# Backward attention: scores and dP on four 32-row strips, one dP tile in 32 multiplied by GpSimd

## The chip, the cores and the metric

One core of a Trainium2 chip runs the whole program in one launch. Time is the device time of one execution in microseconds; the figure compared is the median over runs. The engines are named as the profile names them: PE (TensorE matmul), PEld (its weight loads), DVE (VectorE), ACT (ScalarE), POOL (GpSimd) and SP (SyncE, which here issues DMAs). PSUM is the memory that PE writes; "crossbar" is the DMA path that transposes 128x128 blocks while it copies.

## The reference

The kernel computes the output and nine gradients of a transformer block with adaptive layer norm: x has 2048 tokens of 512 features, attention has 32 heads of 16 features. Cut to the part that the change touches:

```python
def _A_ref(x, wqkv, wo):            # x: 1 x 2048 x 512, H = 32, Dh = 16
    q, k, v = ...                   # each 1 x 32 x 2048 x 16
    scores = jnp.einsum('bhqd,bhkd->bhqk', q, k) * Dh ** (-0.5)
    p = _softmax(scores, axis=-1)
    o = jnp.einsum('bhqk,bhkd->bhqd', p, v)
    return o.transpose(0, 2, 1, 3).reshape(B, S, D) @ wo
...
_out, _vjp = jax.vjp(_f, A_x, A_wqkv, A_wo, B_w1, B_b1, B_w2, B_b2, c, w_mod)
_grads = _vjp(grad_out)
```

The backward pass of attention needs, for each head, the scores again, P = exp(scores) (a division by the row sum is folded into other operands), dP = dO V^T minus the row term, dS = P * dP, and from these dV = P^T dO, dK = dS^T Q and dQ = dS K.

## The kernel before

The program runs in three parts: the forward pass with the MLP and its backward work in the background (`phase_fwd`), the backward pass of attention (`phase5`, with the loops in `attn_bwd`), and the weight gradients and the input gradient (`phase6`). The change lies in `attn_bwd` and in the functions that set up its operands.

**Loops.** The 32 heads form eight groups of four (`g`), each of two pairs (`jp`), and a pair has two heads (`a`). For one pair, `c` runs over four stretches of 512 keys and `ib` over 16 blocks of 128 queries. One (`g`, `jp`, `c`, `ib`) is a *unit*: two tiles of 128 queries by 512 keys, one for each head. There are 8 x 2 x 4 x 16 = 1024 units. Four units in a row (`G` = 4) are a *group* with one `ds` tile of 128 x (4 x 2 x 512); a pair has 16 groups, and there are 256 of them.

**One unit.** For each head `a`:

1. PE multiplies the scores `st` (L1555). Q lies transposed with four heads in 128 partitions, head j in partitions 32j and up. The other operand `masked["KT"][j]` holds K of one head in its rows and zeros elsewhere, and the matmul takes 64 rows.
2. PE multiplies `dp` (L1494) of the unit before, from `dOT` and `masked["VT"][j]`, whose heads lie two strips further on, so that it uses the opposite 64 rows. It has 18 rows a head: 16 features and two for the row term.
3. ACT takes the exponential of `st` into `pu` (L1559).
4. DVE multiplies `dp` by `pu` into `ds` (L1496).

`st` and `dp` have three PSUM buffers each, `pu` six, `ds` three and `dsT` four.

**Behind it.** `dS` puts the unit on the list `pend`; at every second unit `kv_two` takes two units from there and accumulates dK and dV in `acckv` (L1448), two units at four to five units' distance. dQ needs dS with keys in the partitions. That is `dsT`, 32 blocks of 128x128 for a group. The first four blocks (unit 0, head 0) are turned by PE (`turn_ds`, L1513) and copied out of PSUM by ACT (L1514) once the third unit of the group is under way; the other 28 are turned by the crossbar in one DMA that SP issues when the group's last product is done (L1504). `dq` (L1470) takes its units from the list `pendq` two groups later. When a stretch of keys is done ACT copies `acckv` to `kvT` (L1451), and after a pair `turn` transposes that on PE, into an `st` buffer, and ACT copies it out (L1459, L1463).

**Loads.** POOL issues the loads of the next pair and the next group (`pair_pieces`, `load_group`), one for a group of units and 14 in most pairs. Each is preceded by a one-element copy `tick` (L1543) that reads an element of `ds` and so holds POOL until DVE has got there. `pair_pieces` loads K and V of the next pair into the rows of the masked tiles; their other rows were set to zero once, in `open_bwd` (L1375).

**Order.** PE, SP and POOL run in the order in which the program was written, DVE and ACT in the scheduler's.

Of the kernel before, what the change touches and what calls it, by code (L numbers as in the profile page):

```python
# [9 lines left out]
BF16 = mybir.dt.bfloat16  # L10
F32 = mybir.dt.float32
ACT = mybir.ActivationFunctionType
ALU = mybir.AluOpType
# [6 lines left out]
P = 128  # L20
DH = 16
# [84 lines left out]
class K:  # L106
# [1249 lines left out]
    def open_bwd(self):  # L1356

        nc = self.nc
        S, ST, D, DT = self.S, self.ST, self.D, self.DT
        self.open_pool("pad_r", bufs=1, side="right").tile([P, 240], BF16, name="pad_r")  # L1360
        xp = self.open_pool("p5x", bufs=1, side="right")
        self.wp = self.open_pool("p5w", bufs=1, side="right")
        cp = self.open_pool("p5c", bufs=1, side="right")
        m01 = xp.tile([P, 4 * S], BF16, name="m01")
        self.q0 = xp.tile([P, 2 * S + 3 * ST * 4 * DH], BF16, name="q0")
        self.xhat1_6 = m01[:, :ST * D].rearrange("p (st d) -> p st d", d=D)
        self.wq_6 = self.q0[:, :3 * DT * D].rearrange("p (kt n) -> p kt n", n=3 * D)
        nc.vector.memset(self.kvs[0:64], self.scale)
        nc.vector.memset(self.kvs[64:P], 1.0)
        m23 = cp.tile([P, 4 * S], BF16, name="m23")  # L1370
        self.masked = {n: [m[:, (2 * t + a) * S:(2 * t + a + 1) * S] for m in (m01, m23) for a in range(2)]
                       for t, n in enumerate(("KT", "VT"))}
        for ms in self.masked.values():
            for m in ms:
                nc.vector.memset(m, 0.0)  # L1375
        self.qp = self.open_pool("p5q", bufs=1, side="right")
        self.Tq = {}

# [35 lines left out]
    def pair_pieces(self, g, jp):  # L1414
        pieces = []
        for n, src, sh, rows in (("KT", self.KTq_d, 0, DH), ("VT", self.VTq_d, 2, DH + 2)):
            for j in (2 * jp, 2 * jp + 1):
                r = 32 * ((j + sh) % 4)
                pieces.append((self.masked[n][j][r:r + rows, :], src[g, r:r + rows, :]))
        return pieces  # L1420

    def attn_bwd(self):
# [7 lines left out]
        tc, nc = self.tc, self.nc  # L1430
        S, D, H, NQ, ST, SC = self.S, self.D, self.H, self.NQ, self.ST, self.SC
        G = 4
# [3 lines left out]
        acckv = accp.tile([P, 512], F32, name="acckv")  # L1436
        nc.vector.memset(acckv[:], 0.0)
        accq = accp.tile([P, ST, 2, DH], F32, name="accq")
        masked, kvs = self.masked, self.kvs
        pend, pendq = [], []  # L1440

        def kv(u):
# [10 lines left out]
        def turn(g, jp, kvT, s0):  # L1453

            h0 = 4 * g + 2 * jp
            n = ST // 2
            tp = stp.tile([P, n, P], BF16, name="st")
            for st in range(n):
                nc.tensor.transpose(tp[:, st, :], kvT[:, (s0 + st) * P:(s0 + st + 1) * P], self.ident[:])  # L1459
            v = tp[:].rearrange("p s (t a e) -> p t s a e", t=2, a=2)  # L1460
            for t, dst in enumerate((self.dk_t, self.dv_t)):
                d = dst[:, s0:s0 + n, h0 * DH:(h0 + 2) * DH].rearrange("p s (a d) -> p s a d", a=2)
                nc.scalar.copy(d, v[:, t, :, :, 0:DH])  # L1463
# [15 lines left out]
        def kv_two(n=2):  # L1479
            for u in pend[2 - n:2]:  # L1480
                kv(u)
            (T, g, jp, c, ib, kvT, pu, ds) = pend[1]
            del pend[:2]
            if c % 2 and ib == ST - 1 and (g, jp) == (NQ - 1, 1):
                turnq.append((g, jp, kvT, 4 * (c - 1)))
            elif c == SC - 1 and ib == ST - 1:
                turnq.extend((g, jp, kvT, s0) for s0 in (0, ST // 2))

        def dP(u, a):

            (T, g, jp, c, ib, kvT, pu, dsg, i, grp) = u
            rd = slice(64 - 64 * jp, 128 - 64 * jp)
            dp = dpp.tile([P, 512], F32, name="dp")
            nc.tensor.matmul(dp[:], lhsT=T["dOT"][rd, ib * P:(ib + 1) * P],  # L1494
                             rhs=masked["VT"][2 * jp + a][rd, 512 * c:512 * (c + 1)], start=True, stop=True)
            nc.vector.tensor_tensor(dsg[:, i, a], dp[:], pu[:, a, :], ALU.mult)  # L1496

        def dS(u):

            (T, g, jp, c, ib, kvT, pu, dsg, i, grp) = u  # L1500
            pend.append((T, g, jp, c, ib, kvT, pu, dsg[:, i]))
            if i == G - 1:
                dsT = grp[0]
                nc.sync.dma_start_transpose(dsT[:, 4:, :], dsg[:].rearrange("p i a k -> p (i a k)")[:, 512:])  # L1504
                for i in range(G):
                    pendq.append((T, g, jp, c, ib - G + 1 + i, i, dsT))

        def turn_ds(dsg, grp):

            dsT = dtp.tile([P, 8 * G, P], BF16, name="dsT")  # L1510
            tp = stp.tile([P, 4, P], BF16, name="st")
            for b in range(4):
                nc.tensor.transpose(tp[:, b, :], dsg[:, 0, 0, b * P:(b + 1) * P], self.ident[:])  # L1513
            nc.scalar.copy(dsT[:, 0:4, :], tp[:])  # L1514
            grp.append(dsT)

        tick = self.tick
        T = self.T0
        turnq, last = [], None
        for g in range(NQ):  # L1520
            for jp in range(2):
                if jp == 0:
                    if g + 1 < NQ:
                        Tn, later = self.load_group(g + 1)
                    else:
                        Tn, later = None, self.wq_pieces(1) + self.load_wmt()
                    cut = len(later) // 2 if Tn else len(later)
                    pieces = self.pair_pieces(g, 1) + later[:cut]
                    later = later[cut:]
                elif g + 1 < NQ:  # L1530
                    pieces = self.pair_pieces(g + 1, 0) + later
                else:
                    pieces = [(self.xhat1_6[:, st, :], self.xhat1_d.rearrange("(st p) d -> p st d", p=P)[:, st, :])
                              for st in range(ST)]
                kvT = kvp.tile([P, S], BF16, name="kvT")
                total = len(pieces)
                for c in range(SC):
                    c0 = 512 * c
                    for ib0 in range(0, ST, G):
                        m = c * (ST // G) + ib0 // G  # L1540
                        while pieces and (total - len(pieces)) * SC * ST <= m * G * total:
                            if last:
                                nc.gpsimd.tensor_copy(tick[:], last[7][0:1, 0, 0, 0:1])  # L1543
                            nc.gpsimd.dma_start(*pieces.pop(0))
                        dsg, grp = self.dsp.tile([P, G, 2, 512], BF16, name="ds"), []
                        for i in range(G):
                            ib = ib0 + i
                            q = slice(ib * P, (ib + 1) * P)
                            if turnq and i == 2:
                                turn(*turnq.pop(0))  # L1550
                            pu = self.pup.tile([P, 2, 512], BF16, name="pu")
                            for a in range(2):
                                stt = stp.tile([P, 512], F32, name="st")
                                rs = slice(64 * jp, 64 * jp + 64)
                                nc.tensor.matmul(stt[:], lhsT=T["QT"][rs, q], rhs=masked["KT"][2 * jp + a][rs, c0:c0 + 512],  # L1555
                                                 start=True, stop=True)
                                if last:
                                    dP(last, a)
                                nc.scalar.activation(pu[:, a, :], stt[:], ACT.Exp, scale=self.scale)  # L1559
                            if last:  # L1560
                                dS(last)
                            last = (T, g, jp, c, ib, kvT, pu, dsg, i, grp)
                            if i % 2 == 1 and len(pend) >= 4:
                                kv_two()
                            elif i % 2 == 0 and len(pendq) > 2 * G:
                                for _ in range(4 if len(pendq) > 3 * G else 2):
                                    dq(pendq.pop(0), [0, 1])
                            if i == 2:
                                turn_ds(dsg, grp)
            T = Tn  # L1570
        with tc.manual_schedule(engines=ALL):
            for t in (2, 0):
# [338 lines left out]
```

The softmax here doesn't subtract the row's maximum and nothing guards it: scores larger than these inputs give would overflow.

## Time and profile before

| | |
|---|---|
| median of 3 runs | 2569.79 us (2552.87 to 2571.11) |
| span of the profiled execution | 2562.0 us |
| what lies around the span, median less span | 7.8 us |
| PE, PEld busy over the span | 2483.2 us (97%), 1227.4 us (48%) |
| DVE, ACT, POOL busy over the span | 1767.4 us (69%), 2314.2 us (90%), 569.5 us (22%) |
| products `ds` on DVE (L1496) | 2048, from 1180.6 us to 2437.7 us, 677 ns each |
| exponentials `pu` on ACT (L1559) | 2048, 612 ns each |
| crossbar transfers (L1504) | 256, 6.7 us from issue to landing (median), 8.8 at most |
| granted PE clock | 0.994 |

No time of the profiled execution other than its span is recorded; the median stands for it. Busy time counts from an instruction's start to its end, and instructions of one engine overlap by about a tenth of a microsecond, so that an engine that is 97% busy can still have room: the distance from start to start of like instructions shows what it can do. "Idle before" in a group's row is time in which the engine stood still ahead of such an instruction, with what it waited for. The DMA share is a mean over 16 DMA engines and can exceed 1, since packets overlap.

### The profile page before, as it was taken

The page shows a single profiled execution, that of the slowest core. Times are in us where ns is not written, and L with a number is a line of the kernel's source. Part 1 is how long each engine was busy: PE and PEld are TensorE (multiplying, and loading weights), DVE is VectorE, ACT ScalarE, POOL GpSimd, SP SyncE. Part 2 cuts the span into 40 slices and gives each one's busy share as a digit, 9 for nine tenths or more (in the row PEclk, how much of TensorE's full clock was granted, in tenths as well). Part 3 has the DMA queues.
Part 4 walks back from the last instruction along what each step waited for, and adds up shares of the span by engine and source line. Part 5 has one row for each costly group of instructions (what it writes and reads, how often), then busy time and mean ns, then how long its engine had stood idle before and what let it go on. Part 6 is the DMA issues. An engine that isn't in the chain of part 4 may idle for free.

```text
span 2562.0 us, 77852 instructions
## 1 busy us (share of the span) xinstructions
PE 2483.2 (97%) x31239; PEld 1227.4 (48%) x31239; DVE 1767.4 (69%) x3651; ACT 2314.2 (90%) x3757; POOL 569.5 (22%) x1137
## 2 busy tenths in 40 slices
PE   8999899999999999899999999999999999999998
PEld 4555555555555554663444444444444444444443
DVE  6222323323322344667999999999999999999957
ACT  7999999999999996436999999999999999999935
POOL 3554521320221131353011111111111111111223
PEclk9999999999999999999999999999999999999999
DMA  4588742450351153799999999999999999999997
GB/s 165 118 180 196 173 95 83 100 113 22 112 128 49 39 143 113 154 190 211 205 205 202 199 200 201 203 204 200 197 199 198 208 201 197 201 201 229 213 202 191
DMA packets 1193040, 425.37 MB, mean 166 GB/s; under 512 B 1138004, under 2 KB 1161686, under 8 KB 1192678
## 3 DMA queue, kind: packets, MB, share of 16 engines
q1 hardware_dynamic: 1153542, 319.25, 64.2%
q0 software_dynamic: 37056, 100.11, 13.1%
q8 instruction: 244, 4.00, 0.6%
q10 hardware_dynamic: 2080, 1.05, 0.1%
q14 instruction: 118, 0.97, 0.1%
HBM read 73.73 MB, written 62.40 MB: 53 GB/s over the span
## 4 chain that ended last, share of the span: by engine, by line
PE 67%; ACT 20%; DMA 5%; issue 4%; POOL 2%; DVE 1%; SPq 1%; POOLq 0%; DVEq 0%; ACTq 0%
PE st L1555 20%; ACT pu L391 16%; PE acckv L1448 11%; PE accq L1470 8%; PE st L388 7%; PE accbank L322 3%; PE dp L1494 3%; ACT pu L1559 2%; PE st L1513 2%; PE dps L1047 2%; PE pps L1234 2%; PE dp L1604 1%; PE st L1699 1%; DMA dsT<-ds 1%; DMA ev_tm<-ev_fm 1%
## 5 line engine op out<-in xcount | busy, mean ns | idle before, releaser
L1496 DVE TENSOR_TENSOR ds<-dp,pu 128x512 bf16<-128x512 f32 x2048 | 1236.2, 679 | 13.1 <-PE dp L1494 10.2
L1559 ACT ACTIVATE pu<-st 128x512 bf16<-128x512 f32 x2048 | 1073.7, 612 | 46.4 <-PE dp L1494 22.5
L391 ACT ACTIVATE pu<-st 128x1024 bf16<-128x1024 f32 x992 | 912.1, 1077 | 4.6 <-PE st L388 4.4
L388 PE MATMUL st<-QTm,KTq 128*128 128x512 bf16 x1984 | 588.6, 377 | 19.5 <-ACT pu L391 6.0
L322 PEld LDWEIGHTS <-pu 128*128 128x128 bf16 x8192 | 347.5, 96 | 236.1 <-issue 3.1
L322 PE MATMUL accbank<-Vaug,pu 128*128 128x17 bf16 x8192 | 357.7, 171 | 1.2 <-ACT Vaug L522 0.9
L1494 PE MATMUL dp<-m,q 64*128 64x512 bf16 x1024 | 345.7, 382 | 1.1 <-DVE g2w L1053 0.7
L1494 PE MATMUL dp<-m,dOTg 64*128 64x512 bf16 x1024 | 344.6, 381 | 0.1
L1470 PEld LDWEIGHTS <-dsT 128*128 128x128 bf16 x8192 | 239.5, 96 | 213.8 <-issue 209.7
L1555 PE MATMUL st<-m,q 64*128 64x512 bf16 x1024 | 319.5, 382 | 9.2 <-ACT pu L1559 7.5
L1555 PE MATMUL st<-m,QTg 64*128 64x512 bf16 x1024 | 318.9, 381 | 9.5 <-ACT pu L1559 7.8
L388 PEld LDWEIGHTS <-KTq 128*128 128x128 bf16 x1984 | 188.3, 96 | 176.9 <-issue 125.5
L1543 POOL COPY tick<-ds 1x1 bf16<-1x1 bf16 x223 | 39.6, 178 | 1005.4 <-DVE ds L1496 1005.4
L1448 PE MATMUL acckv<-ds,q 128*16 128x512 bf16 x1024 | 154.0, 381 | 0.0
L1448 PE MATMUL acckv<-pu,dOg 128*16 128x512 bf16 x1024 | 154.0, 381 | 0.0
L1448 PE MATMUL acckv<-ds,Qg 128*16 128x512 bf16 x1024 | 154.0, 381 | 0.0
L1448 PE MATMUL acckv<-pu,q 128*16 128x512 bf16 x1024 | 154.0, 381 | 0.0
L1514 ACT COPY dsT<-st 128x512 bf16<-128x512 bf16 x256 | 152.4, 595 | 1.0 <-PE st L1513 1.0
L1470 PE MATMUL accq<-Kg,dsT 128*128 128x16 bf16 x4096 | 143.3, 170 | 3.4 <-DMA dsT<-ds 3.4
L1470 PE MATMUL accq<-q,dsT 128*128 128x16 bf16 x4096 | 143.6, 170 | 0.4 <-DMA dsT<-ds 0.3
L302 POOL DMA_DIRECT2D QTm<-QTq_d x124 | 63.3, 512 | 341.3 <-PE st L388 320.2
L329 DVE RECIPROCAL rl<-accbank 128x4 f32<-128x4 f32 x128 | 22.9, 179 | 162.6 <-PE accbank L322 162.5
(379 smaller groups left out, 2864.8 us busy)
## 6 DMA issues: line engine op xcount, KB each, us to landing
KTq<-KTq_d POOLq DMA_DIRECT2D x24, 512.0 KB, 3.9
duT_d<-auT POOLq DMA_DIRECT2D x3, 1792.0 KB, 7.8
aT_d<-rT POOLq DMA_DIRECT2D x3, 1792.0 KB, 11.1
KTq_d<-KTq SPq DMA_DIRECT2D x32, 128.0 KB, 2.0
QTq_d<-ev_fm SPq DMA_DIRECT2D x32, 128.0 KB, 3.9
VTq_d<-vT POOLq DMA_DIRECT2D x4, 1024.0 KB, 6.8
dsT<-ds SPq DMA_TRANSPOSE x256, 6.7
dx<-dx_d SPq DMA_DIRECT2D x16, 256.0 KB, 4.4
```

The costliest lines, as they stand in the source:

```text
L302: nc.gpsimd.dma_start(QTm[j][32 * j:32 * j + 32, :], self.QTq_d[g, 32 * j:32 * j + 32, 512 * qc:512 * (qc + 1)])
L322: nc.tensor.matmul(acc[:, a, sub, :], lhsT=pu[:, a, sub * P:(sub + 1) * P], rhs=Vaug[:, kb, h, :], start=(kb == 0 and a == 0 and sub == 0) ...
L388: nc.tensor.matmul(stt[:, a, :], lhsT=KT[:, kb * P:(kb + 1) * P], rhs=QTm[2 * jp + a][:], start=True, stop=True)
L391: nc.scalar.activation(pu[:], stt[:], ACT.Exp, scale=self.scale)
L1047: nc.tensor.matmul(pt[:], lhsT=a[st], rhs=g_tm[:, st, :], start=(st == 0), stop=(st == ST - 1))
L1448: nc.tensor.matmul(acckv[r:r + DH, :], lhsT=T[n][:, ib, col:col + DH], rhs=src[:, a, :], start=(ib == 0), stop=(ib == ST - 1))
L1470: nc.tensor.matmul(accq[:, ib, a, :], lhsT=dsT[:, (i * 2 + a) * 4 + sub, :], rhs=T["K"][:, 4 * c + sub, col:col + DH], start=(c == 0 and i ...
L1494: nc.tensor.matmul(dp[:], lhsT=T["dOT"][rd, ib * P:(ib + 1) * P], rhs=masked["VT"][2 * jp + a][rd, 512 * c:512 * (c + 1)], start=True, sto ...
L1496: nc.vector.tensor_tensor(dsg[:, i, a], dp[:], pu[:, a, :], ALU.mult)
L1514: nc.scalar.copy(dsT[:, 0:4, :], tp[:])
L1555: nc.tensor.matmul(stt[:], lhsT=T["QT"][rs, q], rhs=masked["KT"][2 * jp + a][rs, c0:c0 + 512], start=True, stop=True)
L1559: nc.scalar.activation(pu[:, a, :], stt[:], ACT.Exp, scale=self.scale)
```

## The change

- The masked K and V tiles with their zeros go. One tile `KTg` holds K of all four heads of a group, 16 rows in each 32-row strip, and one tile `VTg` holds V with 18 rows. The loads write the same rows from the same sources as before, now of these two tiles. The eight memsets go; 8 KB a partition come free.
- The scores of head j use the 16 rows at 32j; dP uses the 18 rows at 32((j + 2) mod 4). The four matmuls of a unit lie in four different strips. Their order is as before.
- In groups for which `off` holds (the second of every four, 64 of 256), the dP tile of unit 0, head 1 is not multiplied by DVE. ACT copies it to an fp32 tile `dpf` in SBUF, behind the second exponential of the unit that follows (dP lags one unit), and POOL multiplies it by `pu` into `ds`.
- In the same groups the four blocks of unit 0, head 0 are not turned by PE and copied by ACT: the crossbar turns all 32 blocks of the group.

```diff
-        m23 = cp.tile([P, 4 * S], BF16, name="m23")
-        self.masked = {n: [m[:, (2 * t + a) * S:(2 * t + a + 1) * S] for m in (m01, m23) for a in range(2)]
-                       for t, n in enumerate(("KT", "VT"))}
-        for ms in self.masked.values():
-            for m in ms:
-                nc.vector.memset(m, 0.0)
+        self.kvT = {n: cp.tile([P, S], BF16, name=n) for n in ("KTg", "VTg")}
...
-                pieces.append((self.masked[n][j][r:r + rows, :], src[g, r:r + rows, :]))
+                pieces.append((self.kvT[n + "g"][r:r + rows, :], src[g, r:r + rows, :]))
...
         def dP(u, a):
             (T, g, jp, c, ib, kvT, pu, dsg, i, grp) = u
-            rd = slice(64 - 64 * jp, 128 - 64 * jp)
+            r = 32 * ((2 * jp + a + 2) % 4)
             dp = dpp.tile([P, 512], F32, name="dp")
-            nc.tensor.matmul(dp[:], lhsT=T["dOT"][rd, ib * P:(ib + 1) * P],
-                             rhs=masked["VT"][2 * jp + a][rd, 512 * c:512 * (c + 1)], start=True, stop=True)
+            nc.tensor.matmul(dp[:], lhsT=T["dOT"][r:r + DH + 2, ib * P:(ib + 1) * P],
+                             rhs=VTg[r:r + DH + 2, 512 * c:512 * (c + 1)], start=True, stop=True)
+            if a == 1 and i == 0 and off(c, ib):
+                return dp
             nc.vector.tensor_tensor(dsg[:, i, a], dp[:], pu[:, a, :], ALU.mult)
+
+        def off(c, ib):
+            return (c * SC + ib // G) % 4 == 1
+
+        def dP_pool(u, dp):
+            (T, g, jp, c, ib, kvT, pu, dsg, i, grp) = u
+            f = self.dsp.tile([P, 512], F32, name="dpf", bufs=2)
+            nc.scalar.copy(f[:], dp[:])
+            nc.gpsimd.tensor_tensor(dsg[:, i, 1], f[:], pu[:, 1, :], ALU.mult)
 
         def dS(u):
             ...
             if i == G - 1:
-                dsT = grp[0]
-                nc.sync.dma_start_transpose(dsT[:, 4:, :], dsg[:].rearrange("p i a k -> p (i a k)")[:, 512:])
+                dsT, n = grp
+                nc.sync.dma_start_transpose(dsT[:, n:, :], dsg[:].rearrange("p i a k -> p (i a k)")[:, n * P:])
...
-        def turn_ds(dsg, grp):
+        def turn_ds(dsg, grp, skip):
             dsT = dtp.tile([P, 8 * G, P], BF16, name="dsT")
+            grp.extend((dsT, 0 if skip else 4))
+            if skip:
+                return
...
-                                rs = slice(64 * jp, 64 * jp + 64)
-                                nc.tensor.matmul(stt[:], lhsT=T["QT"][rs, q], rhs=masked["KT"][2 * jp + a][rs, c0:c0 + 512],
+                                r = 32 * (2 * jp + a)
+                                nc.tensor.matmul(stt[:], lhsT=T["QT"][r:r + DH, q], rhs=KTg[r:r + DH, c0:c0 + 512],
                                                  start=True, stop=True)
-                                if last:
-                                    dP(last, a)
+                                held = dP(last, a) if last else None
                                 nc.scalar.activation(pu[:, a, :], stt[:], ACT.Exp, scale=self.scale)
+                                if held:
+                                    dP_pool(last, held)
...
-                                turn_ds(dsg, grp)
+                                turn_ds(dsg, grp, off(c, ib))
```

More of the change, by code (lines that the diff above doesn't have):

```diff
@@ L1438, in attn_bwd @@
         accq = accp.tile([P, ST, 2, DH], F32, name="accq")
-        masked, kvs = self.masked, self.kvs
+        KTg, VTg, kvs = self.kvT["KTg"], self.kvT["VTg"], self.kvs
         pend, pendq = [], []
@@ L1514, in turn_ds @@
             nc.scalar.copy(dsT[:, 0:4, :], tp[:])
-            grp.append(dsT)
         tick = self.tick
```

## The prediction

> **What bounds the kernel now.** I read the 40 slices first: from 1180 us to 2438 us of the 2562.0 us span PE, VectorE (DVE) and ScalarE (ACT) are all at nine tenths, and the DMA engines too. That is the backward pass over scores, the only stage that the change touches. Its busy times, one row for the stretch (PE, PEld, DVE, ACT, POOL), and the groups in it:
>
> ```profile
> 1180.00:2438.00 1258.00, 1238.17 (x17589) 532.21 (x17589) 1244.40 (x2065) 1225.11 (x2428) 162.37 (x456) 1.00 1.03 203
> ...
> L1496 DVE TENSOR_TENSOR ds<-dp,pu 128x512 bf16<-128x512 f32 x2048 | 1236.2, 679 | 13.1 <-PE dp L1494 10.2 <-issue 0.5
> L1559 ACT ACTIVATE pu<-st 128x512 bf16<-128x512 f32 x2047 | 1073.2, 612 | 25.1 <-PE dp L1494 22.5
> ...
> L1514 ACT COPY dsT<-st 128x512 bf16<-128x512 bf16 x256 | 152.4, 595 | 1.0 <-PE st L1513 1.0
> ```
>
> Busy shares of 97 to 99% on three engines name no bound, because instructions overlap. So I took a timeline of one group (four units of two tiles, 256 groups in all) and looked for the engine that never waits. First DVE and ACT:
>
> ```profile
> 1701.48 6.06 DVE L1496 TENSOR_TENSOR ds<-dp,pu 128x512 bf16<-128x512 f32 x10
> ...
> 1702.16 0.59 ACT L1514 COPY dsT<-st 128x512 bf16<-128x512 bf16 x1
> 1702.64 3.07 ACT L1559 ACTIVATE pu<-st 128x512 bf16<-128x512 f32 x6
> 1705.87 1.08 ACT L1559 ACTIVATE pu<-st 128x512 bf16<-128x512 f32 x2 [0.16 <-PE dp L1494]
> 1706.94 0.59 ACT L1514 COPY dsT<-st 128x512 bf16<-128x512 bf16 x1
> ```
>
> DVE runs ten products in 6.06 us: (6.06 - 0.68) / 9 = 0.598 us from start to start. A group is eight of them, 4.78 us, and that is the distance between the two ACT copies (1706.94 - 1702.16). ACT needs (3.07 - 0.612) / 5 = 0.49 us for an exponential and 0.48 us for the copy: 8 x 0.49 + 0.48 = 4.40 us, with an idle gap. **DVE sets the pace.** Then PE in the same group:
>
> ```profile
> 1702.06 0.39 PE L1555 MATMUL st<-m,QTg 64*128 64x512 bf16 x1
> 1702.06 0.39 PE L1494 MATMUL dp<-m,dOTg 64*128 64x512 bf16 x1
> 1702.28 0.38 PE L1555 MATMUL st<-m,QTg 64*128 64x512 bf16 x1
> 1702.29 0.38 PE L1494 MATMUL dp<-m,dOTg 64*128 64x512 bf16 x1
> 1702.59 0.39 PE L1448 MATMUL acckv<-ds,Qg 128*16 128x512 bf16 x2
> ...
> 1704.43 0.38 PE L1555 MATMUL st<-m,QTg 64*128 64x512 bf16 x1
> 1704.61 0.37 PE L1494 MATMUL dp<-m,dOTg 64*128 64x512 bf16 x1
> ```
>
> Scores and dP on opposite 64-row halves start together; the second pair follows 0.22 us later. At 1704.61 a dP stands 0.18 us behind its partner: it waits for one of three dp buffers, that is for DVE. Unhindered, a group costs PE four times 0.53 us (st to what follows), two kv blocks of 0.54, two dq blocks of 0.50 and a transpose block of 0.34: 4.54 us, only 0.24 under DVE.
>
> The DMA share of 1.03 is not saturation. The same group in steps of 0.4 us (the last two columns are DMA share and GB/s):
>
> ```profile
> 1702.40:1702.80 0.40, 0.40 (x8) 0.11 (x8) 0.40 (x2) 0.40 (x2) 0.00 (x0) 1.00 1.00 223
> 1704.40:1704.80 0.40, 0.40 (x4) 0.00 (x0) 0.40 (x2) 0.40 (x2) 0.00 (x0) 1.00 1.28 292
> 1705.60:1706.00 0.40, 0.40 (x4) 0.00 (x0) 0.40 (x2) 0.24 (x2) 0.12 (x1) 1.00 0.00 0
> 1706.00:1706.40 0.40, 0.40 (x14) 0.30 (x13) 0.40 (x2) 0.40 (x2) 0.14 (x2) 1.00 0.03 8
> ```
>
> The crossbar transfers run at some 290 GB/s and then stand still for about 0.8 us before the next group.
>
> **The change part by part.** *DVE.* Four groups of every 16 give away one tile: 64 of 2048 products. 64 x 0.598 = **38.3 us** off the engine that sets the end. The stage lasts 1257.1 us (first product 1180.6, last ends 2437.7). DVE's own work is 2048 x 0.598 + 16 dq copies x 0.6 = 1234 us, so 23 us are lateness, of which the table of waits names 10.2 us, all on PE dP. Some 12 us of the 23 lie at kvT turns, where eight transposes and two ACT copies hold an st buffer: after 15 of them one product starts about 0.5 us late (at 1264.21 DVE had idled 0.45 us on PE dP) and a next one 0.3, 15 x 0.8. The change leaves these.
>
> *PE.* With four strips all four products of a unit may start together: a unit's 0.53 becomes 0.53 - 0.22 = 0.31, the group 4.54 - 4 x 0.22 = 3.66 us, and 3.32 where the transposes go. PE does not set the end, so this is worth what it removes of the lateness: between 0 and 23 us. I take **8 us**: most of the 23 - 12 that turns don't explain. It also gives room: the new DVE mean of 31 x 0.598 / 4 = 4.63 us would have stood 0.09 above the old PE cost.
> [...]
>
> *ACT.* 64 copies of the turned tile (L1514, 595 ns) go, 64 copies of dP come, fp32 to fp32; the nearest row is L1615, the same shape and types, 587 ns. Sum 0. But in the touched group DVE needs 7 x 0.598 = 4.19 us and ACT still 4.40. With three st and three dp buffers queued the 0.2 us is lent by neighbouring groups, where ACT has 0.38 to spare. Without that cover it is 64 x 0.21 = 13 us.
>
> *The hand-over.* After the skipped tile DVE wants the next dP 0.6 us sooner. At the old pace that dP was issued at 1705.45 and done by 1705.83, while DVE would come free at 1705.80: under 0.1 us. Bounds 0 and 0.1, so 0 to 6 us; I take **5 us** lost, with ACT's part in it.
>
> *POOL.* 64 products of 128x512. The rows: L1054 fp32, 1283 ns, L1147 bf16, 1163 ns; so 74 to 82 us on an engine that is busy 162 of 1258 us. The product is wanted by kv one group later (the list of pending units holds four or five) and by the transfer after three more units, at least 3 us; copy and product take 0.6 + 1.3 us. Behind it on POOL stands the next tick and one load, which get late by up to 1.7 us; a pair has 16 groups for its 14 loads and uses them in the next pair, so nothing waits. If that cover were gone, kv would wait about 1 us a time, 64 us.
> The trace shows POOL multiplying over a DVE product of the kind at issue (one PSUM input):
>
> ```profile
> 1131.56 1.29 POOL L1054 TENSOR_TENSOR dgb_acc<-dgb_acc,g2w 128x512 f32<-128x512 f32 x1
> 1132.10 0.69 DVE L1050 TENSOR_TENSOR dw<-dps,mod 128x512 bf16<-128x512 f32 x1 [0.96 <-PE dps L1047]
> 1132.71 0.68 DVE L1053 TENSOR_TENSOR g2w<-dps,w_blk 128x512 f32<-128x512 f32 x1
> ```
>
> Its 0.69 us are the 689 ns mean of that row, POOL or no POOL, so I charge nothing for contention.
> [...]
>
> *Crossbar.* 32 blocks instead of 28 in 64 groups. A block is 32 KB; four take 131 KB / 290 GB/s = 0.45 us. SP's issue grows from 3.6 (median) to about 4.1 us, inside the 4.2 to 4.4 us of the short group. The transfer issued at 1700.40 is first read by dq at 1708.50, 8.1 us on, and lands after 6.7 (median, 8.8 at most). The touched group lands at 7.2 and is read at 7.6 or later. Cost 0 while that 0.4 us lasts; past it a dq wait of at most 0.5 us a time is still covered by DVE's three queued tiles.
>
> *The rest.* Eight memsets (L1375, 7.3 us of DVE) go from 1050 to 1180 us, where DVE is busy 35 us in 50 and PE 46 to 48: 0, at most 7. The loads keep number and size. The 124 us after the stage are untouched.
>
> **Sum:** 38.3 + 8 - 5 = 41 us. The span is 2562.0 us; the median of the runs, 2569.8, lies 7.8 above, which I take as what surrounds it (the runs scatter from 2552.9 to 2571.1). 2569.8 - 41 = **2529 us**; with the bounds (38 - 13 + 0 to 38 + 23) 2509 to 2545.
>
> **The rivals.** *ACT takes over.* If nothing is lent between groups, a touched group lasts ACT's 4.40 plus 0.1 for a copy that waits for its dP, 4.50: 0.28 saved x 64 = 18 us, **2552**. For it: ACT's margin is a tenth of its time. Against: the gap of 0.16 us in a plain group and the buffers. *Strips don't run side by side,* and scores and dP pair as now: PE keeps 4.54, little lateness goes, 33 us saved, **2537**. *The crossbar's slack is used up* by collisions with loads, and touched groups give back what they save: **2570**. *Slower: the shared tile.* KTg and VTg now hold both pairs' rows, and 60 loads write them while other rows are read. If the guards go by tile and not by partition, PE waits for each landing, 4.7 us in the table of issues, less the 1.8 us of DVE's three tiles: 60 x 2.9 = 174 us, **2703**; it decides as soon as one st waits for a load. Against: the ticks that read one element of ds are released after that element's product while later ones still write the tile, so guards go by region, though this shows it for columns only.
>
> **How the numbers follow.** Forecast 0.62, ACT 0.15, strips 0.08, crossbar 0.06, shared tile or a like wait 0.09. The range 2508 to 2558 holds the first three and leaves out 0.15 above and a little below. A measurement of this kernel tells about 1% (26 us) from no change: faster by more takes the forecast and the strips, 0.70; within it ACT and part of the crossbar, 0.20; slower 0.10.
>
> **What would show it.** Right: 1984 DVE products still 0.6 us apart, the stage near 1216 us, four matmuls of a unit starting within a few ns, touched groups near 4.3 us, ACT's waits for dP smaller, a gap left between transfers. Wrong: L1496 waiting for ACT, POOL or PE by more than 23 us in sum, dq waiting for dsT, st waiting for a load of KTg, or DVE products longer while POOL multiplies.

## The result, and the profile after

| | before | after |
|---|---|---|
| median of 4 runs each | 2563.68 us | 2903.72 us (2900.76 to 2910.95) |
| ratio to before | | 1.134 [1.130, 1.138] |
| span of the profiled execution | 2562.0 us | 2899.3 us |
| first product of the stage begins | 1180.6 us | 1162.2 us |
| stage, first product to the end of the last | 1257.1 us | 1615.3 us |
| mean granted PE clock of the execution | 0.994 | 0.721 |

The change costs 13%, where a gain of 1.6% was forecast. The spans differ by 337.3 us: the stage is 358.2 us longer, begins 18.4 us sooner, and what follows it is 2.5 us shorter.

In the profile after, the row that tells most is one that the prediction never used, the granted clock. Two rows of the 40 slices (each digit a fortieth of the span, in tenths), and the stretch of the stage with its busy times (PE, PEld, DVE, ACT, POOL), granted clock, DMA share and GB/s:

```profile
PE   8999999999999999999999999999999999999998
...
PEclk9999999999999999555555555555555555555589
```

```profile
1168.00:2780.00 1612.00, 1611.18 (x17309) 546.71 (x17306) 1253.52 (x1990) 1261.17 (x2416) 230.55 (x518) 0.50 0.77 164
```

Before, that stretch had a clock of 1.00 and DVE, ACT and PE all busy. Now PE is busy for 1611 of 1612 us, at half the clock; DVE and ACT are idle for some 350 us each. The groups say for whom they wait:

```profile
L1493 DVE TENSOR_TENSOR ds<-dp,pu 128x512 bf16<-128x512 f32 x1984 | 1251.3, 684 | 356.3 <-PE dp L1489 243.2
L1566 ACT ACTIVATE pu<-st 128x512 bf16<-128x512 f32 x2048 | 1103.7, 595 | 327.7 <-PE dp L1489 221.8
L1489 PE MATMUL dp<-VTg,q 18*128 18x512 bf16 x1024 | 399.9, 598 | 1.4 <-DVE g2w L1053 0.9
...
L1502 POOL TENSOR_TENSOR ds<-dpf,pu 128x512 bf16<-128x512 f32 x64 | 73.8, 1153 | 544.3 <-ACT dpf L1501 544.3
```

A matmul takes 598 ns where it took 0.38 to 0.39 us, and PE waits 1.4 us ahead of this group. The bound has moved from DVE to PE. One group of PE, after:

```profile
1703.74 0.60 PE L1563 MATMUL st<-KTg,q 16*128 16x512 bf16 x1
1703.75 0.60 PE L1489 MATMUL dp<-VTg,q 18*128 18x512 bf16 x1
1703.75 0.60 PE L1563 MATMUL st<-KTg,q 16*128 16x512 bf16 x1
1703.75 0.60 PE L1489 MATMUL dp<-VTg,q 18*128 18x512 bf16 x1
1704.29 0.59 PE L1465 MATMUL accq<-q,dsT 128*128 128x16 bf16 x16
1704.74 0.59 PE L1522 MATMUL st<-ident,ds 128*128 128x128 bf16 x4
1705.26 0.60 PE L1563 MATMUL st<-KTg,q 16*128 16x512 bf16 x1
...
1706.11 0.60 PE L1443 MATMUL acckv<-ds,q 128*16 128x512 bf16 x2
...
1707.07 0.60 PE L1563 MATMUL st<-KTg,q 16*128 16x512 bf16 x1
```

The four strips start within 0.01 us of each other, as the change means them to. But the unit then takes 1704.29 - 1703.75 = 0.54 us, no less than the 0.53 of the two staggered pairs before, and everything else on PE is dearer too: kv of two units 1707.07 - 1706.11 = 0.96 us where it took 0.54, the four transposes 1705.26 - 1704.74 = 0.52 where they took 0.32 (1701.74 to 1702.06). From 1703.74 to the same place of the next group (1710.04) it is 6.30 us, where it was 4.78.

When does the clock fall? Here is PE at the start of the stage, in the kernel after and then in the kernel before:

```profile
1161.77 0.38 PE L1563 MATMUL st<-KTg,q 16*128 16x512 bf16 x1
...
1163.70 0.60 PE L1563 MATMUL st<-KTg,q 16*128 16x512 bf16 x1
```

```profile
1181.36 0.37 PE L1494 MATMUL dp<-m,q 64*128 64x512 bf16 x1 [0.33 <-DVE ds L1496]
...
1183.00 0.63 PE L1555 MATMUL st<-m,q 64*128 64x512 bf16 x1
...
1185.43 0.39 PE L1448 MATMUL acckv<-ds,q 128*16 128x512 bf16 x2
```

Both fall to half clock soon after the first unit, where PE does little (after, it is busy for 0.8 of the 1.7 us from 1160.0; before, for 1.4 of the 2.5 us from 1179.4). The kernel before gets the clock back after 3.4 us (0.50 from 1181.94 to 1185.36), once the stage is in full swing. The kernel after does not: the clock's records show half clock from 1163.7 to 2781.6 us but for 3.4 us, and full clock again when the next part begins.

### The profile page after: what moved, and what is told of

It reads as the page before. It is cut to its first block, busy times and chain, and to the rows that moved or that the text cites. A ratio compares the mean times of both kernels' runs of the same rounds, so it can differ in the third digit from the quotient of the medians.

```text
span 2899.3 us, 77301 instructions
## 1 busy us (share of the span) xinstructions
PE 2852.3 (98%) x30983; PEld 1237.2 (43%) x30983; DVE 1775.0 (61%) x3579; ACT 2355.6 (81%) x3757; POOL 638.9 (22%) x1201
## 4 chain that ended last, share of the span: by engine, by line
PE 78%; ACT 17%; issue 2%; DVE 2%; DMA 1%; POOL 0%; ACTq 0%; DVEq 0%; POOLq 0%
PE st L1563 23%; PE acckv L1443 17%; ACT pu L391 16%; PE accq L1465 9%; PE st L388 7%; PE accbank L322 3%; PE st L1522 3%; PE dp L1489 3%; PE dps L992 1%; PE dps L1047 1%; PE dp L1613 1%; PE pps L1234 1%; PE st L1454 1%; PE pps L631 1%; PE st L1708 1%
## 5 line engine op out<-in xcount | busy, mean ns | idle before, releaser
L1489 PE MATMUL dp<-VTg,q 18*128 18x512 bf16 x1024 | 399.9, 598 | 1.4 <-DVE g2w L1053 0.9
L1489 PE MATMUL dp<-VTg,dOTg 18*128 18x512 bf16 x1024 | 399.9, 600 | 0.0
L1563 PE MATMUL st<-KTg,q 16*128 16x512 bf16 x1024 | 366.1, 595 | 0.7 <-ACT pu L1566 0.7
L1563 PE MATMUL st<-KTg,QTg 16*128 16x512 bf16 x1024 | 366.4, 598 | 0.0
L1443 PE MATMUL acckv<-pu,dOg 128*16 128x512 bf16 x1024 | 262.4, 614 | 0.0
L1443 PE MATMUL acckv<-ds,Qg 128*16 128x512 bf16 x1024 | 262.3, 614 | 0.0
L1443 PE MATMUL acckv<-pu,q 128*16 128x512 bf16 x1024 | 261.8, 613 | 0.0
L1443 PE MATMUL acckv<-ds,q 128*16 128x512 bf16 x1024 | 261.7, 613 | 0.0
L1502 POOL TENSOR_TENSOR ds<-dpf,pu 128x512 bf16<-128x512 f32 x64 | 73.8, 1153 | 544.3 <-ACT dpf L1501 544.3
L1563 PEld LDWEIGHTS <-q 16*128 16x128 bf16 x1024 | 53.9, 98 | 228.9 <-issue 224.9
```

Of the source, the lines that this page charges most:

```text
L1443: nc.tensor.matmul(acckv[r:r + DH, :], lhsT=T[n][:, ib, col:col + DH], rhs=src[:, a, :], start=(ib == 0), stop=(ib == ST - 1))
L1489: nc.tensor.matmul(dp[:], lhsT=T["dOT"][r:r + DH + 2, ib * P:(ib + 1) * P], rhs=VTg[r:r + DH + 2, 512 * c:512 * (c + 1)], start=True, stop ...
L1502: nc.gpsimd.tensor_tensor(dsg[:, i, 1], f[:], pu[:, 1, :], ALU.mult)
L1563: nc.tensor.matmul(stt[:], lhsT=T["QT"][r:r + DH, q], rhs=KTg[r:r + DH, c0:c0 + 512], start=True, stop=True)
```

## The theories

Three guesses at what takes the clock away; the two profiles so far show none of them. A: the chip grants the clock by how much of the PE array the matmuls occupy, and matmuls of 16 and 18 rows leave the stage under the mark. B: the four strips running at once are what is throttled. C: the offload (GpSimd's product, the longer crossbar transfer) slows the stage, and the clock follows.

For A, I count the array's occupation in full-array column steps: a matmul of r rows and m columns of the array over n streamed columns is n x (r/128) x (m/128). A unit of the kernel before is 4 x 512 x 64/128 = 1024 for scores and dP, 256 for kv, 128 for dq and 128 for the transposes, 1536 in all. In the kernel after scores and dP are 512 x (2 x 16 + 2 x 18)/128 = 272, and the unit, averaged over groups with and without transposes, about 752.

## Experiments on the clock

**Which half of the change.** The 64-row masked operands come back and the offload stays:

```diff
-            r = 32 * ((2 * jp + a + 2) % 4)
+            rd = slice(64 - 64 * jp, 128 - 64 * jp)
-            nc.tensor.matmul(dp[:], lhsT=T["dOT"][r:r + DH + 2, ...], rhs=VTg[r:r + DH + 2, ...], ...)
+            nc.tensor.matmul(dp[:], lhsT=T["dOT"][rd, ...], rhs=masked["VT"][2 * jp + a][rd, ...], ...)
...     (scores, loads and memsets likewise; dpf is put into self.junk6)
```

> The change without its strips: scores and dP again on 64 rows with zeros, the offload to GpSimd and the 32-block transfer kept (the fp32 copy lies in an idle tile, for want of room). Theory A, the clock gate: 16 and 18 rows of 128 are too little work for whatever grants PE its clock, so the strips alone halve it. Then the granted clock is 1.0 in the stage and the time about 2525 us, the offload's 38 us below before. Theory B, four matmuls at once draw too much and a limiter halves the clock: the same here. Theory C, the offload (its gaps, GpSimd, the longer transfer) upsets PE: clock 0.5 and about 2880 us or more.

And the strips without the offload:

```diff
         def off(c, ib):
-            return (c * SC + ib // G) % 4 == 1
+            return False
```

> The strips without the offload: no group is touched, DVE has all 2048 products and PE all transposes. Theories A and B: clock 0.5 in the stage, about 2904 us plus some 64 transpose blocks at half clock (0.6 us each) = 2940 us. Theory C: clock 1.0, about 2550 us.

e1 took 2554.94 us, 0.9978 [0.9965, 0.9992] of the kernel before, with a clock of 0.998. e2 took 2932.68 us in one run, clock 0.718. The loss is all with the strips, and the offload even takes 29 us off at half clock. C falls. (e1's clock is as A expected, but not its time, 30 us above A's 2525; the next section takes that up.)

**Rows or simultaneity.** First, the same strips with 32 rows instead of 16 and 18; the added rows hold zeros, so that, two memsets aside, nothing but the occupation changes:

```diff
+        for t in self.kvT.values():
+            nc.vector.memset(t[:], 0.0)
...
-            nc.tensor.matmul(dp[:], lhsT=T["dOT"][r:r + DH + 2, ...], rhs=VTg[r:r + DH + 2, ...], ...)
+            nc.tensor.matmul(dp[:], lhsT=T["dOT"][r:r + 32, ...], rhs=VTg[r:r + 32, ...], ...)
...     (scores likewise)
```

> The change, but each strip multiplies all its 32 rows; the rows without data hold zeros in KTg and VTg, so the results are the same. A unit then works 4 x 32 = 128 rows for 512 columns, against 68 in the change and 256 before. Theory A, if rows are counted one by one: the clock rises, to 1.0 (about 2525 us) if 128 is enough, and stays 0.5 (2904 us) if not; if strips are counted, no difference, 2904 us. Theory B: no difference or worse, 2904 us.

Second, the kernel after with one more matmul in every unit, over the whole array. The scores' own matmul overwrites its output, so it is nothing but load:

```diff
+                                if a == 0:
+                                    nc.tensor.matmul(stt[:], lhsT=T["Q"][:, 0:2, :]..., rhs=T["K"][:, 0:8, :]..., ...)
```

> The change plus one useless 128x128x512 matmul a unit, written to the st buffer and overwritten by the scores: 1024 matmuls of extra work for PE. A unit then works 68 + 128 = 196 rows. Theory A: more work wakes the clock, 1.0 in the stage, about 2530 us, faster than the change by 370. Theory B and C: the clock stays at 0.5, and 1024 x 0.43 us are added, about 3340 us.

One run each. e3: 2879.11 us, clock 0.74, and 6% of the stage at full clock. e4: 2648.04 us, clock 0.989. **Giving PE more to do made the kernel 256 us faster.** The stretch of the stage in e4:

```profile
1164.00:2514.00 1350.00, 1348.84 (x18318) 537.42 (x18316) 1247.22 (x1999) 1238.08 (x2426) 230.29 (x519) 0.98 0.96 195
```

The strips still start together there (at 1702.07 and 1702.08 in one unit), so B falls: with the same four at once, and more work besides, the clock of the stage is 0.98 where it was 0.50. The time is 118 us above A's 2530: PE is busy for 1349 of 1350 us, so that with the dense matmuls PE sets the pace.

**How much is enough.** The next kernels step through the occupation. e6 adds to e3 kv matmuls that take 32 columns of the array instead of 16 (`lhsT=T[n][:, ib, col - a*DH : col - a*DH + 32]`, accumulated in 32 rows of `acckv`); e7 is e6 with the offload in the fourth group of four instead of the second (`off` compares with 3).

> Strips of 32 rows with zeros, as in the run that gave 2879 us, and the kv products take 32 columns (both heads of the pair, of which one is used) instead of 16, at the same number of instructions and columns streamed. The work of a unit in full-array steps is 512 (scores, dP) + 512 (kv) + 128 (dq) + 96 (turn) = 1248, against 992 there, 752 in the change, 1264 with the dense extra matmul and 1536 before. Theory A with rows times columns counted: as with the dense extra matmul the clock goes to 1.0, and without its 1024 x 0.22 us the time is 2545 to 2560 us. Rows alone counted: no difference, 2879 us.

> The same with the offload in the fourth of every four groups. Theories A and D together: clock 1.0, no stalls at kvT, PE with room, 2510 to 2525 us, the fastest so far. A wrong on columns: 2879 us. E: as the run with the second group, 2545 to 2560.

e6 took 2872.64 us in one run, with 11% of the stage at full clock. e7 took 2808.7 us, from 2724.21 to 2833.15 over four runs, and 29% in the profiled one: the clock goes to and fro and the time with it. Had the columns counted as the rows do, both would have stood at 1248 steps, beside e4's 1264 at full clock; so the columns of kv count little or not. (The two differ in the offload's place alone; e7's times spread over 109 us, so that 11% against 29% can be scatter.)

e8 breaks the simultaneity instead: scores on 64 masked rows, dP on strips of 18.

```diff
-                                nc.tensor.matmul(stt[:], lhsT=T["QT"][r:r + DH, q], rhs=KTg[r:r + DH, c0:c0 + 512], ...)
+                                nc.tensor.matmul(stt[:], lhsT=T["QT"][rs, q], rhs=mK[2 * jp + a][rs, c0:c0 + 512], ...)
```

> Half of the strips undone: scores on 64 rows with zeros, dP on 18-row strips, offload as in the change. Work of a unit: 512 + 144 + 256 + 224 = 1136 full-array steps, between the 992 that gave a clock of 0.5 nearly throughout and the 1264 that gave 1.0. Theory A (a threshold on work): a clock between, more than half of the stage at 1.0, 2560 to 2700 us. Theory B (simultaneous matmuls): at most three run together; if three suffice to halve the clock, 2880 us, if not 2555.

It took 4362.48 us in one run, by far the slowest, at half clock throughout, where A, going by the steps of a unit, expected more than half of the stage at full clock. Its timeline shows what that left out:

```profile
1701.16 0.60 PE L1567 MATMUL st<-m,QTg 64*128 64x512 bf16 x1
1701.69 0.60 PE L1493 MATMUL dp<-VTg,dOTg 18*128 18x512 bf16 x1
1702.23 0.60 PE L1567 MATMUL st<-m,QTg 64*128 64x512 bf16 x1
1702.77 0.60 PE L1493 MATMUL dp<-VTg,dOTg 18*128 18x512 bf16 x1
1703.30 0.35 PE L1469 MATMUL accq<-Kg,dsT 128*128 128x16 bf16 x7
```

Matmuls of 64 and of 18 rows don't run beside each other here, though they lie on different rows: 0.54 us from start to start, 2.14 us for the four. So the steps of a unit are spread over twice the time (3.00 us a unit, 1.58 in the kernel after). None of the four runs beside another here and the clock is at 0.50 all the same, which is a second blow to B. Why the four stand one behind another the rows don't show.

The last three kernels give back half of e4's load: the dense matmul in every second unit only (`if a == 0 and i % 2 == 1`), with 32-row strips (e9, offload as in e7; e11, no offload) and with the change's own 16 and 18 rows (e10, offload as in e7).

> Strips of 32 rows with zeros, the offload in the fourth of every four groups, and the useless dense 128x128x512 matmul at every second unit only, right behind dq, which uses the whole array too. Work of a unit: 512 + 256 (dense, half) + 256 (kv) + 224 = 1248 full-array steps, near the 1264 that held the clock. PE at full clock: 3.66 us a group and two dense matmuls of 0.22, 4.1 us, under DVE's 4.63. Theory A: clock 1.0 and 2515 to 2540 us, at or below the 2547 of the offload on 64 rows, because the next dP comes 0.2 us earlier behind a touched tile. Theory B (four at once): 0.5 and about 3000 us.

> The same with the 16 and 18 rows of the change. Work of a unit: 272 + 256 + 256 + 224 = 1008, like the 992 of 32-row strips alone. Theory A: clock at 0.5 for most of the stage, 2850 to 3050 us (the dense matmuls cost 512 x 0.43 us more there). If the dense matmul wakes the clock by being dense and not by the sum of work: 1.0, 2530 us.

> The first of these three without the offload: what strips alone bring at full clock. DVE has 2048 products, 1234 us of own work. Theory A with DVE as the bound: 2550 to 2565 us, the lateness of 23 us shrunk by 0 to 10. Theory B: 0.5, 3050 us.

e9 took 2576.8 us, 1.0065 [1.0045, 1.0084] of the kernel before; e11 2576.52 us, 1.0058 [1.0041, 1.0075]; e10 2868.13 us in one run. The stretch of the stage in e9, and then in e10:

```profile
1170.00:2448.00 1278.00, 1267.01 (x17795) 515.63 (x17796) 1227.91 (x1996) 1222.59 (x2424) 227.49 (x513) 0.99 1.05 206
```

```profile
1170.00:2750.00 1580.00, 1575.41 (x17826) 527.11 (x17826) 1268.14 (x1989) 1262.02 (x2416) 230.68 (x516) 0.60 0.82 167
```

The clock is as A expected in all three; the times of e9 and e11 lie 37 and 12 us above their ranges. e9 and e10 issue the same instructions for scores, dP and load; they differ in the rows of zeros that the strips take along, 32 against 16 and 18, and in the two memsets for them. The rows decide between a clock of 0.99 and one of 0.60, and with it 290 us.

All of it in one table (the stage over 1024 units gives the time of a unit; the steps leave the extra columns of kv out):

| kernel | steps a unit | steps per us | share of the stage at full clock |
|---|---|---|---|
| e8 | 1136 | 379 | 0.1% |
| after | 752 | 477 | 0.3% |
| e2 | 784 | 491 | 0.1% |
| e3 | 992 | 638 | 6% |
| e6 | 992 | 643 | 11% |
| e10 | 1008 | 652 | 20% |
| e7 | 992 | 680 | 29% |
| e4 | 1264 | 958 | 97% |
| e9 | 1248 | 998 | 99% |
| e11 | 1280 | 1021 | 100% |
| e1, e12, e5 | 1504 | 1227 to 1237 | 100% |
| before | 1536 | 1251 | 99.7% |

**A is shown in its direction**: more occupied rows go with more of the clock, from 0.3% of the stage in the kernel after over 6% in e3 to 100% in e1, and from 20% in e10 to 99% in e9, whatever runs at once (e11's strips start four at a time at full clock, as the rows further down show) and with the offload or without (e2, e11); only e8, whose matmuls don't run side by side, doesn't fit. What exactly the chip counts is open. The steps of a unit alone don't order the kernels (e8, e10). Steps per us do, but for spells of a few us (after, e2, before); but a kernel that gets the clock also does more per us, so that column is partly a consequence; and no run lies between 680 and 958.

That consequence can be taken out by counting the units that begin under each clock. At half clock e8 does 379 steps per us and after 476, and they stay there (after but for 3.4 us); e3, e6, e7 and e10 do 614 to 625 and get the full clock now and then; e4 does 699 and gets it after 44 us, e9 777 and gets it after 7. At full clock e3, e6, e7 and e10 do 801 to 822 and lose it again each time, within 126 us at most; e4 does 967 and e9 1000, and of these e9 loses it once, for 7 us. So in these kernels a higher rate goes with getting the clock sooner and, on the whole, with keeping it longer, as A has it; whether there are fixed marks, and where, these runs don't say.

## Experiments on the rest of the sum

**What the offload is worth at full clock.** DVE's lateness is the stage less 0.598 us for each of its products. It was 1257.1 - 2048 x 0.598 = 32.4 us before (the prediction's 23 us leave out the 16 dq copies). e1 has 64 products fewer, 38.3 us of them, yet its stage is 1255.4 us: lateness 1255.4 - 1984 x 0.598 = 69.0 us. Nearly all that was given away came back as waiting. The table of waits of e1 from 1250 to 2400 us (us in sum, times, longest), then DVE and ACT where the longest kind of them falls:

```profile
DVE ds L1498 <- PE dp L1494: 25.2, 59, 1.2
...
DVE ds L1498 <- ACT junk L1506: 16.7, 16, 1.0
```

```profile
1707.37 18.94 DVE L1498 TENSOR_TENSOR ds<-dp,pu 128x512 bf16<-128x512 f32 x31 [0.49 <-PE dp L1494]
1727.35 4.93 DVE L1498 TENSOR_TENSOR ds<-dp,pu 128x512 bf16<-128x512 f32 x8 [1.04 <-ACT junk L1506]
```

```profile
1726.64 0.66 ACT L1506 COPY junk<-dp 128x512 f32<-128x512 f32 x1
1727.10 0.47 ACT L1463 COPY dk_t<-st 128x256 bf16<-128x256 bf16 x1
1727.37 0.49 ACT L1463 COPY dv_t<-st 128x256 bf16<-128x256 bf16 x1
```

The table puts 16 waits of 1.04 us down to ACT's copy of dP (here into `junk`), which ends just before DVE starts and stands ahead of ACT's copies of the turned kvT of the pair before. But in all 16 DVE starts 0.53 us after the start of its own dP matmul, as in nearly all of the waits that the table puts down to dP, in the kernel before too. So it is dP that is late, and PE shows why: it stands behind a kv block and the eight transposes of kvT.

```profile
1725.72 0.39 PE L1448 MATMUL acckv<-ds,Qg 128*16 128x512 bf16 x2
...
1726.27 0.62 PE L1459 MATMUL st<-ident,kvT 128*128 128x128 bf16 x8
1726.82 0.39 PE L1494 MATMUL dp<-m,dOTg 64*128 64x512 bf16 x1
```

In the kernel before the same 16 products (15 of them in the second group of a pair) are 0.53 us late already; a tile less for DVE only makes that wait longer. Taken over the 64 products that follow a skipped tile, the lateness is 44.4 us, 0.69 us each, where the same products have 8.5 us before. Read at first as a collision on ACT, this led to e5, which moves the offload to the fourth group of four, away from that place:

```diff
         def off(c, ib):
-            return (c * SC + ib // G) % 4 == 1
+            return (c * SC + ib // G) % 4 == 3
...     (otherwise e1)
```

> The offload on 64 rows as before, but in the fourth of every four groups and not the second. In the run with 64 rows and the second group DVE stood still up to 1.04 us in a touched group, where ACT also copies kvT and, after a pair, the two turned tiles. Theory D, collision of ACT's extra copies: away from kvT the stalls go and the stage gets its 38 us, about 2525 us. Theory E, the skipped tile itself starves DVE wherever it stands (PE on 64 rows or ACT can't follow): about 2555 us again.

e5 took 2547.35 us, 0.9957 [0.9944, 0.997] of the kernel before: a little faster than both kernels, and between D's 2525 and E's 2555. Its stage is 1245.1 us, lateness 58.7 us; after the skipped tile it is 20.6 us now, 0.32 each (0.1 us in sum at these products before), and the waits put down to `junk` fall from 16.7 to 1.2 us. So D had the place right, but that ACT's extra copies were the cause isn't shown. What is left there is again dP. DVE, POOL and PE around one skipped tile in e5:

```profile
1701.18 5.47 DVE L1498 TENSOR_TENSOR ds<-dp,pu 128x512 bf16<-128x512 f32 x9 [0.23 <-PE dp L1494]
```

```profile
1701.47 1.15 POOL L1507 TENSOR_TENSOR ds<-junk,pu 128x512 bf16<-128x512 f32 x1 [4.23 <-ACT junk L1506]
```

```profile
1699.80 0.37 PE L1494 MATMUL dp<-m,dOTg 64*128 64x512 bf16 x1
1700.11 0.39 PE L1448 MATMUL acckv<-ds,Qg 128*16 128x512 bf16 x2
...
1700.65 0.39 PE L1494 MATMUL dp<-m,dOTg 64*128 64x512 bf16 x1
```

DVE starts 1701.18 - 1700.65 = 0.53 us after the start of its dP, and that dP stands behind the kv block, which PE issues ahead of it in the written order. No run moves kv, so that this is the cause is read from the rows, not tested. The strips, at full clock, don't cure it: in e9 the products after a skipped tile are 0.31 us late each. And e9 and e11 differ by the offload alone, and their stages by 1280.5 against 1283.2 us, 2.7 of the 38.3. The dense matmul may be in the way there too: ACT waited 35.8 us for scores between 1250 and 2400 us in e11 (29.0 in e9).

**What the memsets cost.** The stage of the kernel after began 18.4 us sooner. To take out what came earlier, I measure from a small memset (L965) to the first product: 159.7 us before, 152.8 in e1 and 152.9 in e5, which also have the eight memsets of the masked tiles; 142.5 in the kernel after and 143.5 in e2, which have none. The kernels between fit: 146.0 to 150.0 in the five with two such memsets on DVE (e3, e6, e7, e9, e11), 151.8 in e8 with four. Why the kernel before has 6.9 us more than e1 and e5 with the same memsets is open; each figure is of one execution. In the kernel before, DVE and PE there read:

```profile
1080.14 0.35 DVE L1006 SCALAR_TENSOR_TENSOR dw<-dps,opcbT,t 128x128 bf16<-128x128 f32 x1 [3.99 <-DMA out_dram<-dw]
...
1081.33 0.91 DVE L1375 MEMSET m<- 128x1024 uint32 x1 [0.16 <-issue]
1082.16 0.23 DVE L1008 SCALAR_TENSOR_TENSOR junk<-dps,w_blk 128x128 bf16<-128x128 f32 x1
```

```profile
1084.14 1.44 PE L992 MATMUL dps<-tm_blk,xh 128*128 128x128 bf16 x12 [6.85 <-DVE junk L1008]
1085.38 0.63 PE L992 MATMUL dps<-tm_l,xh 128*128 128x128 bf16 x4
```

The memsets stand ahead of the small reductions that free PE's accumulators. PE waits 6.85 us (in which DVE itself waits 3.99 us for a DMA of `dw`), and then finds itself at half clock (twelve matmuls take 1.44 us; at full clock 0.83). So the last kernel is e5 with the memsets on GpSimd:

```diff
-                nc.vector.memset(m, 0.0)
+                nc.gpsimd.memset(m, 0.0)
```

> e5_rows64_offload_last with one edit: the eight memsets of the masked tiles (L1375) run on GpSimd in place of VectorE. From the one-element-small memset of L965 to the first product of the stage 159.7 us pass in the kernel before, 152.9 in e1 and in e5, which also have the eight memsets, and 142 to 143.5 in the kernel after, in e2, e4 and e10, which have none. Theory M (the prediction's 0 for the memsets was wrong: on DVE they stand ahead of the reductions that PE waits for): the distance falls from 152.9 to about 143 to 146 us, the stage stays at 1245 us, and the ratio to the kernel before falls from 0.9957 to about 0.992. Rival N (the memsets cost nothing, the earlier start comes from elsewhere): 152.9 us and 0.9957. Rival L (on GpSimd they hold up the loads behind them, GpSimd being busy 38 of 65 us there): the distance grows beyond 153 us and the ratio is above 0.997.

It took 2542.36 us, as theory M had it: 0.9928 [0.9905, 0.995]: the fastest of all the kernels run. The distance is 146.0 us, the stage 1246.7. The same 40 us before the stage, in the kernel before and in e12 (the second number is PE's busy time, the third from the end the granted clock):

```profile
1060.00:1100.00 40.00, 30.46 (x472) 29.89 (x470) 27.36 (x146) 12.88 (x43) 15.13 (x23) 0.87 0.79 148
```

```profile
1060.00:1100.00 40.00, 37.72 (x643) 37.06 (x641) 27.12 (x173) 18.37 (x61) 33.76 (x39) 1.00 1.08 194
```

PE idles 2.3 us instead of 9.5 and keeps the clock. The 6.9 us less than e5 in the distance are in the profiles, one of each; the intervals of the two ratios just overlap (e12's ends at 0.995, e5's begins at 0.9944), so by the ratios alone e12 is not proved faster than e5.

## Why the prediction was wrong

**The step that failed** is the cost of PE: "a unit's 0.53 becomes 0.53 - 0.22 = 0.31, the group 4.54 - 4 x 0.22 = 3.66 us". At full clock that price of a unit is right: in e11 the strips of a unit start at 1702.58 and kv follows at 1702.90, 0.32 us:

```profile
1702.58 0.39 PE L1568 MATMUL st<-KTg,QTg 32*128 32x512 bf16 x1
...
1702.59 0.38 PE L1491 MATMUL dp<-VTg,dOTg 32*128 32x512 bf16 x1
1702.90 0.39 PE L1445 MATMUL acckv<-ds,Qg 128*16 128x512 bf16 x2
```

(Four one after another at the prediction's 0.22 us would be 0.88, so the gain is 2.75 times, counted to the start of kv. The old group was rather 4.44 than 4.54: in the rows of before dq ahead of the transposes takes 0.42 us and they 0.32.) But it was taken from rows at a clock of 1.00 and carried over to a kernel that does half the work on PE, as though the clock belonged to the chip and not to the load. At the granted half clock the unit is 0.54 and the group 6.30 us, against DVE's 4.63, and "between 0 and 23 us" of relief became a loss of 358. The range could not hold it, since no term of the sum had the clock in it.

The trace of before did show that the clock can fall in this very stage: the rows at 1183.00 and 1185.43 above. The prediction passes over them and never asks what holds the clock up here, and whether the change takes that away.

**The rivals.** The slower one named the wrong mechanism. The loads of the shared tiles cost little: the table of waits from 1250 to 2700 us has one row that names them,

```profile
PEld L1443 <- DMA VTg<-VTq_d: 6.7, 11, 0.6
```

6.7 us in sum where it was priced at 174. "Strips don't run side by side" fell with the first timeline. The ACT rival and the crossbar rival can't be read from a kernel whose PE is late. In e5, at full clock and with the same work on ACT, DVE's waits put down to ACT add up to 2.9 us between 1250 and 2400 us, so ACT did not take over there; the crossbar shows in part (below).

**The other terms.**
- *DVE, 38.3 us.* 1984 products at 0.598 us hold in e1, e5 and e9. They shorten the stage only by what isn't waited for instead.
- *The hand-over, 5 us, bounds 0 and 6.* Mis-sized: 44.4 us in e1 (8.5 of them there before), 20.6 in e5, with 64-row operands. The working compared the end of one dP with one DVE end at the old pace (under 0.1 us). But a DVE that waits starts 0.14 us behind that end (1701.18 against 1700.65 + 0.39), and it left out the places where dP stands behind the transposes of kvT as well.
- *Lateness relief, 8 us.* It was to come from strips at full clock, and no run has these without a dense matmul in their way; e11, strips and no offload, has 1283.2 - 2048 x 0.598 = 58.5 us of lateness, more than the 32.4 before. With 64 rows, less what follows a skipped tile, e1 has 24.6 and e5 38.1 us, where the same products have 23.9 and 32.3 before.
- *Memsets, 0, at most 7.* Taken too low: from e5 to e12 they cost 6.9 us, by one execution of each, though they add up to 7.3 us of DVE and DVE was far from full there. "DVE is busy 35 us in 50" says nothing of who waits for the reduction behind them.
- *POOL, 0.* Held: 64 products, 73.8 us, 1153 ns each, predicted 74 to 82; DVE's products are no longer for it: in e5 POOL's of 1.15 us runs beside the nine shown above, which are (5.47 - 0.68) / 8 = 0.60 us apart.
- *Crossbar, 0.* Nearly: waits of PE and PEld for `dsT` from 1250 to 2400 us add up to 0.5 us before, 12.0 in e1 and 11.9 in e5, 25 waits of at most 1.2 us in e5. How much of that reached DVE wasn't separated.

## What to carry to other kernels

Before changing how much work PE does, ask what clock it is granted and whether the leaner version is granted it too: a matmul over 512 columns took 0.38 to 0.39 us before and 0.60 after, so its duration could not be carried over. Look at the PEclk row first, and if PE is nearly 100% busy with a digit of 5 there, the remedy may be more rows, even rows of zeros: e9 has a clock of 0.99 in the stage where e10 has 0.60, and takes 290 us less. And taking an instruction off the engine that sets the pace gains only what its supplier, in the order that it is issued in, can deliver sooner: 2 us of 38 in e1, 12 in e5. Before blaming the engine that a table of waits names, compare the starts: here the product came 0.53 us after the start of its dP, though ACT was named.

## What the runs showed of the hardware that I had not expected

- **A PE that is busy all the time can sit at half clock.** 1611 us of 1612 busy, clock 0.50, so the profile's busy share does not tell the clock. Rows of zeros count as work (e9 against e10, clock 0.99 against 0.60); the doubled columns of kv count little or not (e6, 11% of the stage at full clock against e3's 6%).
- **Useless work can pay:** one dense matmul a unit, 0.31 us each in e11's timeline (1702.27 to 1702.58), brought e4 256 us. It still leaves e4, e9 and e11 slower than before, where the 64 masked rows have a clock of 1.00 in the stage without an instruction of their own.
- **Matmuls of 64 and of 18 rows on different rows didn't run side by side** (e8, 0.54 us from start to start at half clock), while two of 64 rows do (before, at 1185.98 both), and four of 16 and 18 or of 32 in 32-row strips (after, from 1703.74 to 1703.75; e11, from 1702.58 to 1702.59).
